# A route's product one step behind its spread, with two tile buffers, and gathers six units ahead

## The chip, the cores and the metric

The kernel runs on one core of a Trainium2 chip. The metric is device time in microseconds of one execution, from the first to the last instruction with what lies around them; smaller is better. Engines are named as in the profile: PE (TensorE, with PEld for its weight loads), DVE (VectorE), ACT (ScalarE), POOL (GpSimd) and SP (SyncE).

## The reference

```python
N, deg, C, L, DE = 10000, 64, 64, 1, 4      # nodes, mean degree, channels
E = N * deg                                 # 640000 edges
M = (L + 1) ** 2                            # 4 components

def reference(x, src, dst, Y, edge_feat, w_rad, cg, w_mix):
    N, C, M = x.shape[0], x.shape[1], x.shape[2]
    R = _silu(edge_feat @ w_rad)                              # (E, C)
    xs = x[src]                                               # (E, C, M)
    tp = jnp.einsum('eci,ef,ifo->eco', xs, Y, cg)             # (E, C, M)
    msg = R[:, :, None] * tp
    agg = _segment_sum(msg.reshape(-1, C * M), dst, N).reshape(N, C, M)
    return jnp.einsum('ncm,cd->ndm', agg, w_mix)
```

`src` and `dst` are random node numbers, `Y` and `edge_feat` have 4 numbers for each edge, and all data is float32.

## The kernel before

The work is to sort the edges by destination, so that the edges of 32 destination nodes (a bucket) lie together, and then to gather the source rows and add the messages up by matmuls. The edges are taken in two parts, 49% and 51%. Each edge is carried as 9 words (a key of source and destination, `Y`, `edge_feat`).

**Two sorting passes.** Pass 1 (`pass1`, key `grp`) puts a part's edges into 18 groups of 576 nodes; pass 2 (`pass2`, key `bkt`) puts a group's edges into its 18 buckets. Both use `route`, which works on chunks of 12 tiles of 128 edges. Its steps for chunk `k`:

- `prepare`, `places`, `placed`, `slots` find each edge's row and slot, for two chunks at a time (DVE one-hots, PE prefix matmuls, ACT and DVE on their result).
- `spread` (L445 to L467) builds the tiles `X` (the edge's words at its slot, DVE, L453) and `oh` (one-hot of its row: seven of twelve by DVE, L460, five by ACT, L465 and L466). They are rotating buffers; `self.xb` says how many.
- `move` (L469) multiplies them on PE into PSUM: 12 float32 matmuls, recorded as 24 (L473).
- `evict` (L476) copies the PSUM tile to `rt` on ACT (L478). There are `rt_bufs` of them: 6 in the main phase.
- `store` (L480) writes the rows out by an indirect DMA that POOL issues (L481).

In step `k` of the loop, `evict(k-3)` and `move(k-2)` come first and `spread(k)` after them. In the main phase `grp` has two buffers of `X` and `oh`, and `bkt` has three. In the sort of the first part, ahead of the main phase, there are three.

Before a route can start, its table has to be there. In pass 1 `front` counts digits: for each block of 24 tiles a DVE one-hot `Da` (L543), a PE count `cnt` (L546) and, a step later, a DVE addition to `cs` (L550). After that `tables` runs as a chain of short DVE, PE and ACT operations, among them `offp` (L313), `ovp` (L363) and `dp` (L380). PE's results of these share one PSUM bank (`misc`) with the last mixing product `po` (L795); `bank()` hands it out. `weave` lays the next front's steps between the steps of the running route.

**Messages** (`messages`, L668). A unit is half of a bucket's edges in a part: 4 tiles in the first part, 5 in the second; each part has 313 buckets, so 626 units. For unit `k` POOL issues one gather for each tile (L709, into `xg`, with `LG + 2` buffers, `LG` units ahead). PE transposes the payload (`turn`, L722) and makes the radial product (`radial`, L732), and ACT applies SiLU (L735). DVE builds the selection `S` (`spots`, L742 and L745) and multiplies the gathered rows in place (`products`, L752). PE adds up (`sums`, L763). Every fourth bucket is mixed by `wf` (L795) and written out. A unit's work is issued in four quarters:

```python
        quarters = (((index, LI), (gather, LG), (turn, 2), (sums, 0), (silu, 1)), ((turned, 2), (spots, 1)),
                    ((products, 1), (evict, 0)), ((radial, 2), (full, -1)))
```

The PSUM tile of `turn(k+2)` is the one that `products(k)` reads last.

**The order.** `run` first sorts part 0 by pass 1. The main phase, `groups` (L830), then goes through all 36 segments (part and group). Between the quarters of the messages it deals out steps of pass 2 for the next segment (`pass2_steps` over the quarters of the present one) and steps of pass 1 of part 1 (`rate` steps for each quarter, up to the last segment of part 0). In the main phase the program order of PE, DVE and ACT is as written; the scheduler orders POOL and SP by its own reckoning. Each engine works its queue off in order. After the main phase two short loops treat edges that had no place (`overflow`).

Of the kernel before, what the change touches and what calls it, by code (L numbers as in the profile page):

```python
# [17 lines left out]
F = mybir.dt.float32  # L18
# [6 lines left out]
P = 128  # L25
# [7 lines left out]
BT = 18  # L33
UT = 5
SPLIT = ((0.49, 2, 4), (0.51, 2, 5))
LG = 4
LI = 8
LS = 8
BIG = 16384.0
# [30 lines left out]
class Kernel:  # L70
# [320 lines left out]
    def route(self, ps, quad, nt, sb, idx):  # L391

        nc, wk, tc, T, Q = self.nc, self.ph, self.tc, ps.T, ps.Q
        assert Q == 2
        N = (nt + T - 1) // T
        QD, PS, PP, MS, XO, PR, RT = {}, {}, {}, {}, {}, {}, {}

        def prepare(q):
            QD[q] = quad(q * Q * T, min(Q * T, nt - q * Q * T))

        def places(q):
            t0 = q * Q * T
            m = min(Q * T, nt - t0)
            pp = self.ps.tile([P, 28, B], F, name="pp", tag="pos", bufs=1)
            Dq = QD[q][0]
            for c in range((m + T - 1) // T):
                a, z = c * T, min((c + 1) * T, m)
                nc.tensor.matmul(pp[:, a:z, :], ps.identr[:N, q * Q + c:q * Q + c + 1].to_broadcast([N, P]),
                                 sb[:N, :].unsqueeze(1).to_broadcast([N, z - a, B]),
                                 start=(c == 0), stop=False)  # L410
            full = m // T
            if full:
                po = pp[:, :full * T, :].rearrange("p (c t) b -> p c t b", t=T)
                pi = Dq[:, :full * T, :].rearrange("p (c t) b -> p c t b", t=T)
                for u in range(T - 1):
                    k = T - 1 - u
                    nc.tensor.matmul(po[:, :, u + 1:, :], self.onesb,  # L417
                                     pi[:, :, u:u + 1, :].to_broadcast([P, full, k, B]), start=False, stop=False)
            for u in range(full * T, m - 1):
                nc.tensor.matmul(pp[:, u + 1:m, :], self.onesb, Dq[:, u:u + 1, :].to_broadcast([P, m - u - 1, B]),  # L420
                                 start=False, stop=False)
            nc.tensor.matmul(pp[:, :m, :].rearrange("p t b -> p (t b)"), self.A,
                             Dq.rearrange("p t b -> p (t b)"), start=False, stop=True)
            PS[q] = pp

        def placed(q):
            m = min(Q * T, nt - q * Q * T)
            pp = PS.pop(q)
            pc = PP[q] = wk.tile([P, Q * T, B], F, name="pc", tag="pc" + ps.key, bufs=1)
            nc.scalar.activation(pc[:, :m, :], pp[:, :m, :], AF.Copy, bias=-BIG)  # L430

        def slots(q):
            pp = PP.pop(q)
            m = min(Q * T, nt - q * Q * T)
            pos = wk.tile([P, 28], F, name="pos", tag="pos" + ps.key)
            nc.vector.tensor_reduce(pos[:, :m], pp[:, :m, :], axis=AX.X, op=OP.max)
            ri = wk.tile([P, 28], I32, name="row", tag="row" + ps.key)
            nc.vector.tensor_scalar(ri[:, :m], pos[:, :m], 1.0 / ps.r, 0.5 / ps.r - 0.5, op0=OP.mult, op1=OP.add)
            row = wk.tile([P, 28], F, name="rowf", tag="rowf" + ps.key)
            nc.vector.tensor_copy(row[:, :m], ri[:, :m])  # L440
            slot = wk.tile([P, 28], F, name="slot", tag="slot" + ps.key)
            nc.vector.scalar_tensor_tensor(slot[:, :m], row[:, :m], -float(ps.r), pos[:, :m], op0=OP.mult, op1=OP.add)
            MS[q] = (row, slot)

        def spread(c):  # L445
            row, slot = MS[c // Q]
            a = (c % Q) * T
            m = min(T, nt - c * T)
            msk = self.vmsk[:, :m * ps.r].rearrange("p (t s) -> p t s", s=ps.r)
            nc.vector.tensor_tensor(msk, self.v128[:, :ps.r].unsqueeze(1).to_broadcast([P, m, ps.r]),  # L450
                                    slot[:, a:a + m].unsqueeze(2).to_broadcast([P, m, ps.r]), op=OP.is_equal)
            X = self.ph.tile([P, T, ps.rw], F, name="X", tag="X" + ps.key, bufs=self.xb[ps.key])
            nc.vector.tensor_tensor(  # L453
                X[:, :m, :].rearrange("p t (s w) -> p t s w", w=W),
                msk.unsqueeze(3).to_broadcast([P, m, ps.r, W]),
                QD[c // Q][1][:, a:a + m, :].unsqueeze(2).to_broadcast([P, m, ps.r, W]), op=OP.mult)
            oh = self.ph.tile([P, T, P], F, name="oh", tag="oh" + ps.key, bufs=self.xb[ps.key])
            v = max(m - ps.act, 0)
            if v:
                nc.vector.tensor_tensor(oh[:, :v, :], self.v128.unsqueeze(1).to_broadcast([P, v, P]),  # L460
                                        row[:, a:a + v].unsqueeze(2).to_broadcast([P, v, P]), op=OP.is_equal)
            if m - v:
                sq = self.ph.tile([P, 5, P], F, name="sq")
                for u in range(v, m):
                    nc.scalar.activation(sq[:, u - v, :], self.i128, AF.Square, bias=row[:, a + u:a + u + 1], scale=-1.0)  # L465
                nc.scalar.activation(oh[:, v:m, :], sq[:, :m - v, :], AF.Relu, bias=self.ones[:, 0:1], scale=-2.0)  # L466
            XO[c] = (X, oh, m)  # L467

        def move(c):  # L469
            X, oh, m = XO.pop(c)  # L470
            pr = self.ps.tile([P, 512], F, name="pr", tag="route", bufs=2)
            for u in range(m):
                nc.tensor.matmul(pr[:, :ps.rw], oh[:, u, :], X[:, u, :], start=(u == 0), stop=(u == m - 1))  # L473
            PR[c] = pr

        def evict(c):  # L476
            rt = RT[c] = self.ph.tile([P, ps.rw], F, name="rt", tag="rt" + ps.key, bufs=self.rt_bufs)
            nc.scalar.activation(rt, PR.pop(c)[:, :ps.rw], AF.Copy)  # L478

        def store(c):  # L480
            st = nc.gpsimd.indirect_dma_start(  # L481
                out=ps.dst, out_offset=bass.IndirectOffsetOnAxis(ap=idx[:, c:c + 1], axis=0),
                in_=RT.pop(c), in_offset=None, bounds_check=ps.rows - 1, oob_is_err=False)
            if self.in_group[ps.key]:
                tc.declare_no_dep(st.ins, group=ps.key, reason="the rows of a pass are apart")
            tc.add_to_no_dep_group(ps.key, st.ins)
            self.in_group[ps.key] += 1


        for k in range(-2 * Q, N + LS):  # L490
            if 0 <= k - 3 < N:
                evict(k - 3)
            if 0 <= k - 2 < N:
                move(k - 2)
            if k % 2 and 0 <= k + 3 < N:

                while self.pos:
                    yield "held"
                self.pos = True
                places((k + 3) // 2)  # L500
            if k % 2 == 0 and 0 <= k + 2 < N:
                placed((k + 2) // 2)
                self.pos = False
            if k % 2 == 0 and 0 <= k + 4 < N:
                prepare((k + 4) // 2)
            if 0 <= k < N:
                spread(k)
            if (k + 1) % 2 == 0 and 0 <= k + 1 < N:
                slots((k + 1) // 2)
            if 0 <= k - LS < N:  # L510
                store(k - LS)
            yield

    def pass1(self, part, first, size):
# [16 lines left out]
        def front(o, m):  # L531
# [8 lines left out]
            for a in range(0, m, QT):  # L540
                z = min(a + QT, m)
                D = ph.tile([P, QT, B], BF, name="Da", bufs=2)
                self.onehot(D[:, :z - a], da[:, a:z], z - a)  # L543
                yield from self.bank()
                cnt = self.ps.tile([P, 512], F, name="cnt", tag="misc", bufs=1)
                self.count(cnt, ps, D, a // T, z - a, N, True, True)  # L546
# [283 lines left out]
    def groups(self):  # L830
# [11 lines left out]

        total = max(ends[self.NG - 2] - 8, 1) if self.NG > 1 else 1
        nch = (self.part[1][1] - self.part[1][0] + self.p1.T - 1) // self.p1.T
        rate = (nch + 6 * (LS + 4) + 60) / total
        acc = acc1 = 0.0
        i = start = 0
        for v in range(4 * u):
# [106 lines left out]
    def run(self):  # L955
# [2 lines left out]
        self.segs = [(k, g) for k in range(2) for g in order]  # L958
        with tile_pool(name="p1", bufs=2) as self.ph:
            self.rt_bufs = 38  # L960
            self.xb = {"grp": 3}
            self.z = self.ph.tile([P, 2048], F, name="z", bufs=1)
            nc.gpsimd.memset(self.z, 0.0)
            self.consts()
# [9 lines left out]
                run(weave(first, later, 0.25))  # L974
        with tile_pool(name="p2", bufs=2) as self.ph:
            self.rt_bufs = LS - 2
            self.xb = {"grp": 2, "bkt": 3}
            with self.tc.manual_schedule(engines={mybir.EngineType.PE, mybir.EngineType.DVE,
                                                  mybir.EngineType.Activation}):
                self.groups()  # L980
# [32 lines left out]
```

## Time and profile before

| | |
|---|---|
| median of 3 runs | 10404.88 us (10403.27 to 10411.17) |
| profiled execution | 10414.15 us, its span 10412.3 us |
| mean granted TensorE clock | 0.883 |
| pass 1 of part 0, table and sort of the first segment | 0 to about 1130 us |
| main phase with pass 1 of part 1 in it | 1130 to about 5550 us |
| main phase with pass 2 alone beside the messages, last units of part 0 | 5550 to about 6010 us |
| the same, units of part 1 | 6010 to 10256 us |
| end of the last units, overflow loops | 10256 to 10412 us |

A row of the waits names the engine and line that waited, what it waited for, the total in microseconds, how often, and the longest. A row of the groups gives busy time and mean nanoseconds of one, then the idle time before and what ended it. A row of the timeline gives start, duration, engine, line, operation, tiles and shapes, a count where neighbours are merged, and idle time before it in brackets.

### The profile page before, as it was taken

The numbers are of one execution on the slowest core, as the hardware profiler recorded it, in microseconds if no ns is written. First come the engines' busy times: TensorE is split into PE (matmuls) and PEld (weight loads), VectorE is DVE, ScalarE is ACT, GpSimd is POOL, SyncE is SP. The second block draws the span as 40 slices with busy tenths as digits, with TensorE's granted clock in tenths as the row PEclk, the third lists the DMA queues.
The fourth block names the chain that finished last, engine by engine and source line by source line (L and its number), as shares of the span: only waits on it lengthen the run. The fifth ranks groups of instructions, "written<-read, shape, count | busy, mean of one in ns | idle before, by whom it ended". The sixth has DMA issues, their size and how long they took to land. (4 is left out here: it accounts for less than half of the span.)

```text
span 10412.3 us, 159949 instructions
## 1 busy us (share of the span) xinstructions
PE 8505.1 (82%) x58324; PEld 7273.0 (70%) x58324; DVE 7312.6 (70%) x12462; ACT 3587.7 (34%) x11277; POOL 6285.0 (60%) x6576
## 2 busy tenths in 40 slices
PE   6897878778888778878889888888888888888874
PEld 5786767667667667667767677777767777777663
DVE  8998877677677677677767676666666666666643
ACT  3675433233334233334433232222222232332210
POOL 1222655546456446456557777777777777777773
PEclk9998989889889789889889898888899898888986
DMA  3331322223223223223223333333333333333331
GB/s 95 85 91 51 93 74 82 78 64 92 68 71 96 70 65 97 64 70 93 78 76 104 109 109 113 111 112 111 112 112 112 112 111 112 111 111 111 109 112 52
DMA packets 531585, 963.05 MB, mean 92 GB/s; under 512 B 229053, under 2 KB 329720, under 8 KB 530800
## 3 DMA queue, kind: packets, MB, share of 16 engines
q0 software_dynamic: 300464, 790.37, 26.0%
q1 hardware_dynamic: 227744, 149.89, 5.4%
q10 hardware_dynamic: 2592, 12.60, 0.3%
q8 instruction: 459, 7.52, 0.3%
q14 instruction: 326, 2.67, 0.1%
HBM read 830.53 MB, written 131.52 MB: 92 GB/s over the span
## 5 line engine op out<-in xcount | busy, mean ns | idle before, releaser
L709 POOL DMA_INDIRECT xg<-in_x_dram,sidx x5634 | 5359.0, 951 | 2576.7 <-issue 1494.7
L763 PE MATMUL G<-S,xg 128*128 128x128 f32 x22536 | 3329.7, 313 | 5.8 <-DVE dv L742 2.7
L763 PEld LDWEIGHTS G<-S,xg 128*128 128x128 f32 x22536 | 3218.0, 228 | 24.1 <-issue 4.2
L473 PE MATMUL pr<-X,oh 128*128 128x126 f32 x21180 | 2644.8, 282 | 148.1 <-DVE oh L460 85.9
L473 PEld LDWEIGHTS pr<-X,oh 128*128 128x128 f32 x21180 | 2525.4, 197 | 278.6 <-DVE oh L460 97.5
L752 DVE TENSOR_TENSOR xg<-xg,pre 128x1024 f32<-128x1024 f32 (+1 forms) x1252 | 1689.0, 1349 | 1403.3 <-DMA xg<-in_x_dram,sidx 1130.9
L453 DVE TENSOR_TENSOR X<-dv,Wt 128x1512 f32<-128x1512 f32 (+2 forms) x905 | 1531.4, 1692 | 892.0 <-PE pr L473 846.1
L465 ACT ACTIVATE sq<-i,rowf 128x128 f32<-128x128 f32 x4457 | 1397.6, 393 | 60.0 <-DVE rowf L440 49.4
L722 PE MATMUL pre<-ident,pay 128*36 128x128 f32 (+1 forms) x1252 | 402.3, 321 | 1034.8 <-DVE xg L752 1013.2
L735 ACT ACTIVATE pre<-pre 128x256 f32<-128x256 f32 (+1 forms) x1252 | 494.0, 395 | 2000.7 <-PE pre L732 1944.9
L722 PEld LDWEIGHTS pre<-ident,pay 128*36 128x36 f32 (+1 forms) x1252 | 141.0, 113 | 1473.3 <-DVE xg L752 1299.2
L745 DVE TENSOR_TENSOR S<-dv,pay 128x512 f32<-128x512 f32 (+1 forms) x1252 | 949.3, 758 | 223.2 <-PE G L763 133.0
L732 PE MATMUL pre<-wr,sT 36*128 36x256 f32 (+1 forms) x2504 | 1024.4, 492 | 13.6 <-ACT sT L727 13.6
L481 POOL DMA_INDIRECT grp<-rt,idx x417 | 412.5, 989 | 959.2 <-ACT rt L478 563.3
L466 ACT ACTIVATE oh<-sq,ones 128x640 f32<-128x640 f32 (+1 forms) x905 | 740.0, 818 | 620.8 <-PE pr L473 602.1
L460 DVE TENSOR_TENSOR oh<-dv,rowf 128x896 f32<-128x896 f32 x887 | 948.1, 1069 | 0.0
L727 ACT ACTIVATE sT<-pre 36x128 f32<-36x128 f32 (+1 forms) x1252 | 332.4, 265 | 1570.1 <-PE pre L722 1568.3
L481 POOL DMA_INDIRECT bkt<-rt,idx x488 | 487.1, 998 | 458.6 <-ACT rt L478 280.3
L795 PE MATMUL po<-wf,Gs 128*128 128x256 f32 (+2 forms) x2784 | 681.0, 400 | 65.9 <-DVE cs L550 63.5
L795 PEld LDWEIGHTS po<-wf,Gs 128*128 128x128 f32 (+2 forms) x2784 | 509.2, 188 | 227.9 <-DVE cs L550 68.9
L780 ACT ACTIVATE Gs<-G 128x128 f32<-128x128 f32 x1252 | 276.0, 272 | 1068.8 <-PE G L763 1068.7
L417 PE MATMUL pp<-D,onesb 128*128 128x396 bf16 (+14 forms) x4983 | 540.7, 257 | 12.6 <-DVE D L284 12.6
(176 smaller groups left out, 5041.4 us busy)
## 6 DMA issues: line engine op xcount, KB each, us to landing
xg<-in_x_dram,sidx POOLq DMA_INDIRECT x5634
bkt<-z SPq DMA_DIRECT2D x26, 972.0 KB
out_dram<-ot SPq DMA_DIRECT2D x138, 128.0 KB
pay<-bkt SPq DMA_DIRECT2D x17, 810.0 KB
grp<-z SPq DMA_DIRECT2D x17, 738.0 KB
Wt<-grp SPq DMA_DIRECT2D x17, 738.0 KB
grp<-z ACTq DMA_DIRECT2D x17, 706.5 KB
Wt<-grp SPq DMA_DIRECT2D x17, 706.5 KB
```

What stands on the lines that cost most here:

```text
L453: nc.vector.tensor_tensor(X[:, :m, :].rearrange("p t (s w) -> p t s w", w=W), msk.unsqueeze(3).to_broadcast([P, m, ps.r, W]), QD[c // Q][1 ...
L460: nc.vector.tensor_tensor(oh[:, :v, :], self.v128.unsqueeze(1).to_broadcast([P, v, P]), row[:, a:a + v].unsqueeze(2).to_broadcast([P, v, P ...
L465: nc.scalar.activation(sq[:, u - v, :], self.i128, AF.Square, bias=row[:, a + u:a + u + 1], scale=-1.0)
L466: nc.scalar.activation(oh[:, v:m, :], sq[:, :m - v, :], AF.Relu, bias=self.ones[:, 0:1], scale=-2.0)
L473: nc.tensor.matmul(pr[:, :ps.rw], oh[:, u, :], X[:, u, :], start=(u == 0), stop=(u == m - 1))
L481: st = nc.gpsimd.indirect_dma_start(out=ps.dst, out_offset=bass.IndirectOffsetOnAxis(ap=idx[:, c:c + 1], axis=0), in_=RT.pop(c), in_offset ...
L709: nc.gpsimd.indirect_dma_start(out=xg[:, t, :], out_offset=None, in_=self.x, in_offset=bass.IndirectOffsetOnAxis(ap=si[:, u:u + 1], axis=0))
L732: nc.tensor.matmul(R, ST_.pop(k)[:ut * W], self.wr[:ut * W, :ut * 64], start=True, stop=True)
L745: nc.vector.tensor_tensor(S[:, :ut], self.eq[:, :ut].unsqueeze(3).to_broadcast([P, ut, NB, 4]), pb[:, :, 1:5].unsqueeze(2).to_broadcast([P ...
L752: nc.vector.tensor_tensor(V, V, R.unsqueeze(3).to_broadcast([P, ut, 64, 4]), op=OP.mult)
L763: nc.tensor.matmul(G[:, h].rearrange("p n f -> p (n f)"), V[:, t, 32 * h:32 * h + 32, :].rearrange("p c i -> p (c i)"), S[:, t].rearrange( ...
L795: nc.tensor.matmul(po[:nn, :256], Gs[:, h, f].rearrange("p b n -> p (b n)")[:, :nn], self.wf[:, h, f, :], start=(h + f == 0), stop=(h + f ...
```

## The change

- `self.xb` becomes one number for both passes: 3 in the first sort, 2 in the main phase. The distance from spread to product is `lag = xb - 1`: two steps in the first sort, as it was, and one step in the main phase. The eviction stays one step behind the product.
- In `front` a `yield` stands between the block's one-hot and its count, so that the two are a step apart. The rate at which pass 1 of part 1 is dealt out counts 80 further steps instead of 60.
- `LG` is 6 instead of 4: gathers are issued 6 units ahead, into 8 buffers instead of 6.

```diff
-LG = 4
+LG = 6
...
-            X = self.ph.tile([P, T, ps.rw], F, name="X", tag="X" + ps.key, bufs=self.xb[ps.key])
+            X = self.ph.tile([P, T, ps.rw], F, name="X", tag="X" + ps.key, bufs=self.xb)
...
-            oh = self.ph.tile([P, T, P], F, name="oh", tag="oh" + ps.key, bufs=self.xb[ps.key])
+            oh = self.ph.tile([P, T, P], F, name="oh", tag="oh" + ps.key, bufs=self.xb)
...
+        lag = self.xb - 1
         for k in range(-2 * Q, N + LS):
-            if 0 <= k - 3 < N:
-                evict(k - 3)
-            if 0 <= k - 2 < N:
-                move(k - 2)
+            if 0 <= k - lag - 1 < N:
+                evict(k - lag - 1)
+            if 0 <= k - lag < N:
+                move(k - lag)
...
                 self.onehot(D[:, :z - a], da[:, a:z], z - a)
+                yield
                 yield from self.bank()
                 cnt = self.ps.tile([P, 512], F, name="cnt", tag="misc", bufs=1)
...
-        rate = (nch + 6 * (LS + 4) + 60) / total
+        rate = (nch + 6 * (LS + 4) + 80) / total
...
-            self.xb = {"grp": 3}
+            self.xb = 3
...
-            self.xb = {"grp": 2, "bkt": 3}
+            self.xb = 2
```

## The prediction

> **What bounds the kernel now.** I read the page first, then the busy times by stretch, then the waits of each engine inside the stretch that the change touches, then the timeline.
>
> ```profile
> span 10412.3 us, 159949 instructions
> PE 8505.1 (82%) x58324; PEld 7273.0 (70%) x58324; DVE 7312.6 (70%) x12462; ACT 3587.7 (34%) x11277; POOL 6285.0 (60%) x6576
> ...
> 700.00:800.00 100.00, 94.47 (x821) 86.38 (x820) 98.59 (x186) 76.58 (x229) 25.16 (x26) 1.00 0.26 86
> ...
> 1130.00:5550.00 4420.00, 3633.66 (x24723) 3107.61 (x24721) 3150.63 (x5478) 1594.13 (x5115) 2441.89 (x2545) 0.87 0.27 79
> 5550.00:6010.00 460.00, 388.42 (x2677) 330.06 (x2678) 326.39 (x556) 153.41 (x498) 342.00 (x359) 0.91 0.37 106
> 6010.00:10256.00 4246.00, 3535.05 (x23384) 3002.43 (x23384) 2752.70 (x4069) 1177.02 (x3695) 3214.92 (x3370) 0.89 0.38 112
> ```
>
> The rows by stretch give length, then busy time (count) of PE, PEld, DVE, ACT, POOL, then PE's clock. No engine is full on average, but the stretches differ. The sort of the first half (the row at 700) is DVE's: 98.59 of 100. From 1130 to 5550 three things are woven: messages of the first half, pass 2, and pass 1 of the second half. I call it stretch 1; nobody is full there: PE is idle for 4420 − 3634 = 786 us, DVE for 1269. From 5550 on pass 1 is over, and from 6010 (stretch 3) the second half's messages run.
>
> ```profile
> POOL xg L709 <- PE G L763: 773.5, 237, 12.7
> POOL xg L709 <- issue: 531.1, 1727, 3.4
> ...
> L481 POOL DMA_INDIRECT grp<-rt,idx x213 | 214.0, 1005 | 201.0 <-ACT rt L478 88.0 <-issue 44.8 <-DVE S L745 16.0
> L481 POOL DMA_INDIRECT bkt<-rt,idx x210 | 208.7, 994 | 292.5 <-ACT rt L478 230.7 <-issue 22.6 <-DVE S L745 8.2
> ...
> DVE xg L752 <- DMA xg<-in_x_dram,sidx: 1005.3, 304, 6.7
> ```
>
> The first four rows are waits and groups of stretch 1, the last is a wait of stretch 3. Between two gathers lie 531.1 / 1727 = 0.31 us of issue, so one indirect DMA takes 342.00/359 + 0.31 = 1.26 us of POOL. 3370 of them make 4246 us: exactly stretch 3. There POOL is full, its end is POOL's, and DVE's 1005 us of waiting for gathers only show it. In the 460 us before, 359 × 1.26 = 452: full too. So time can be won in stretch 1 alone, and there 773.5 us of POOL's slack (waiting for a gather buffer, that is, for the sums) are the most that can go before POOL is full as well: 4420 − 773 = 3647.
>
> Why PE idles in stretch 1, and what DVE and ACT wait for there:
>
> ```profile
> PE pre L722 <- DVE xg L752: 322.2, 121, 10.1
> PE cnt L291 <- DVE Da L284: 195.2, 61, 11.2
> PE po L795 <- DVE cs L550: 63.5, 23, 3.1
> PE ovp L363 <- DVE rk L360: 53.2, 10, 11.7
> PE pr L473 <- ACT rt L478: 47.2, 64, 3.6
> PE offp L313 <- DVE R L310: 35.9, 9, 8.0
> PE dp L380 <- DVE val L377: 32.0, 8, 6.4
> ...
> PE pr L473 <- DVE oh L460: 0.4, 1, 0.4
> ...
> DVE X L453 <- PE pr L473: 832.4, 204, 10.6
> ...
> DVE xg L752 <- DMA xg<-in_x_dram,sidx: 38.3, 21, 2.9
> ...
> ACT oh L466 <- PE pr L473: 602.1, 185, 15.3
> ```
>
> The seven long rows of PE come to 749 of its 786 us, and six of them wait for DVE. DVE, which is busy only 71% of the stretch, comes late because it stood 832 us at X, 204 times, about once for each of the 213 pass 1 chunks: with two buffers, the spread of chunk k overwrites what the product of k−2 reads, and that product is queued in the very same step. ACT stands there too (602), and the SiLU and the evictions queue behind it.
>
> **The change, part by part.**
>
> *Product one step behind, two buffers.* For pass 1 the product of k−2 now stands one step before spread k. The code deals pass 1 out at (213 + 72 + 60)/2308 = 0.149 steps a quarter unit, one in 6.7 quarters; 530 units in 4420 us are 8.34 us a unit, 2.08 a quarter, so the step is 14 us ahead, more than the longest wait of 10.6. Most of the 832 and 602 go. For pass 2 (three buffers, two steps, to two buffers, one step) the overwrite distance stays one step. What is late next is PE itself: DVE's idle time is worth only what PE waits for DVE. Of the 322.2 at the transpose (it stands before the sums, and both need the product of DVE) I let 60% go, −190 (bounds 0 and −322): of DVE's 1269 idle us 832, 66%, lie at X, and part of its lateness is its own bursts of work. Of the chain waits (63.5 + 53.2 + 35.9 + 32.0 = 184.6), where PE waits for short DVE operations behind a backlog, half, −90 (bounds 0 and −185). The 47.2 for the PSUM buffer stays, since the eviction moves up with the product; a chunk's output tile is still reused six chunks later, and its store keeps its place.
>
> *What it can cost: the product waiting for its own spread.* At lag one the product takes the place that the product of the chunk before has now. Three pass 2 chunks of the timeline:
>
> ```profile
> 3045.66 1.73 DVE L453 TENSOR_TENSOR X<-dv,Wt 128x1512 f32<-128x1512 f32 x1
> 3047.31 1.08 DVE L460 TENSOR_TENSOR oh<-dv,rowf 128x896 f32<-128x896 f32 x1
> 3048.82 0.69 DVE L745 TENSOR_TENSOR S<-dv,pay 128x512 f32<-128x512 f32 x1
> 3049.43 1.21 DVE L752 TENSOR_TENSOR xg<-xg,pre 128x1024 f32<-128x1024 f32 x1
> 3050.56 0.33 DVE L450 TENSOR_TENSOR dv<-dv,slot 128x168 f32<-128x168 f32 x1
> 3052.18 2.84 PE L473 MATMUL pr<-X,oh 128*128 128x126 f32 x24
> 3052.65 1.08 DVE L460 TENSOR_TENSOR oh<-dv,rowf 128x896 f32<-128x896 f32 x1
> 3058.19 1.08 DVE L460 TENSOR_TENSOR oh<-dv,rowf 128x896 f32<-128x896 f32 x1
> 3059.09 2.84 PE L473 MATMUL pr<-X,oh 128*128 128x126 f32 x24
> 3064.10 2.94 PE L473 MATMUL pr<-X,oh 128*128 128x126 f32 x24
> ...
> PE pr L473 <- DVE oh L460: 83.8, 104, 9.1
> ```
>
> The spreads end at 3048.39, 3053.73 and 3059.27; the products one place ahead start at 3052.18, 3059.09 and 3064.10: 3.8, 5.4 and 4.8 us later. So the spread would be in time. Bounds: 0.4 us in all (stretch 1 at lag two, row above) and the last row, the first sort, where DVE is full: 83.8 us for 204 chunks, 0.41 each, for 423 chunks 174. I take +30, near the lower end.
>
> *The yield between the count's one-hot and its matmul.* The count now stands a step (14 us) behind DVE's one-hot instead of right at it: of 195.2 us (61 waits, 3.2 each) 20 stay, −175 (bounds 0 and −195). The longer front takes 10 to 20 more steps a piece; the pace goes from 345 to 365 per 2308 quarters, so pass 1 ends where it did.
>
> *PE's clock.* A wait is paid twice:
>
> ```profile
> 3012.76 1.95 PE L763 MATMUL G<-S,xg 128*128 128x128 f32 x16
> ...
> 3017.47 0.29 PE L722 MATMUL pre<-ident,pay 128*36 128x128 f32 x1 [2.14 <-DVE xg L752]
> 3017.60 2.92 PE L763 MATMUL G<-S,xg 128*128 128x128 f32 x16
> ...
> L763 PE MATMUL G<-S,xg 128*128 128x128 f32 x8480 | 1291.8, 318 | 1.0 <-ACT Gs L780 1.0
> L473 PE MATMUL pr<-X,oh 128*128 128x126 f32 x9814 | 1246.5, 286 | 48.0 <-ACT rt L478 47.2 <-DVE oh L460 0.4
> ```
>
> The same sums took 1.95 us, and 2.92 after a wait of 2.14. The granted clock was 0.87 in stretch 1 with PE idle 18%, and 1.00 at 700 to 800 with PE idle 6%. At full clock 530 units of sums would be 530 × 1.95 = 1034 instead of 1291.8, and 9814/24 = 409 products of 2.84 us 1161 instead of 1246.5: 343 us slow time beside 786 idle, 0.44 for each. The net of the parts so far, −190 − 90 + 30 − 175 = −425, brings −185 more (bounds 0 and −343). The Trainium skill (TensorE: Matmul & The Clock Gate, Part 1: The HAM clock gate) lets the clock fall only after an idle window of about 3.4 us; the mean wait, 322.2/121 = 2.7, is shorter, and by that the −185 would be nothing. The row with 2.14 us speaks against it here.
>
> *POOL fills up.* 4420 − 610 = 3810 against POOL's 3647: 96% full. DVE's wait for gathers is 38.3 us now, at 83%, and 1005.3 where POOL is full. I take +120 (bounds 0 and 1005 × 3810/4246 = 902), near the lower end, since two more units lie ready.
>
> *Gathers 6 ahead, 8 buffers.* The SBUF of one X and one-hot set becomes two gather buffers. In stretch 1 it adds nothing beyond that; at its end POOL is 2 units, 8 gathers × 1.26 = 10 us, further on, and since POOL alone counts from there, −10 at the end. A store that POOL's queue holds behind two more units of gathers lands 2 × 4246/626 = 13.6 us later in stretch 3, and ACT's evictions, with the SiLU queued behind them, may then wait for an output tile. The 4246 − 3535 = 711 us that PE is idle there cover that; without this cover, 13.6 us in each of 17 groups would be 231.
>
> *First sort.* It keeps three buffers and lag two. Its third front is now longer than the route it is woven into (some 107 steps, of which the weave deals out 0.72 × 106 = 76), so part of it and the table chain may lie open:
>
> ```profile
> 1022.35 0.50 DVE L306 TENSOR_REDUCE n<-cs 14x18 f32<-14x216 f32 x1 [1.00 <-ACT cs L653]
> 1040.02 0.18 DVE L387 TENSOR_SCALAR idx<-dest 128x14 int32<-128x14 f32 x1 [0.65 <-ACT dest L384]
> ```
>
> An open table chain took 18 us. I take +15 (0 to 26).
>
> **Sum.** Stretch 1: −425 − 185 + 120 = −490. With −10 and +15: −485. The profiled execution took 10414.15 us (span 10412.3 and 1.9 around it): 9929. The median of the runs, 10404.88, lies 9 below it: **9920 us**.
>
> **Rivals.** (1) *DVE's wait only moves*: freed at X, DVE waits elsewhere for PE, and PE's transposes wait as before; only the counts gain, −175 × 1.44 = −252: 10150. For it: DVE was never full. Against: the late DVE rows. (2) *POOL becomes the bound in stretch 1*: all of its 773 go: 10405 − 773 − 10 + 15 = 9637. It needs nearly all PE idle time to vanish. (3) *Slower: products wait for their spreads.* A group's sort is paced to 52 steps (6 + 14 + 8 + 24) in the 144 quarters of 36 units, so a pass 2 step is 2.77 × 2.08 = 5.8 us. If DVE has spots, product and a pass 1 spread (0.69 + 1.21 + 3.14, the last being 0.33 + 1.73 + 1.08) in front of its own 3.14, it takes 8.2: 2.4 us of waiting for each of 210 chunks, 504, with the clock's 1.44 726: 10405 − 485 + 726 = 10646. It ends slower than before when the mean wait exceeds 485/(210 × 1.44) = 1.6 us. Against: the 3.8 to 5.4 us above. (4) *No difference*: gains and costs cancel, or stretch 1 is paced by something these views do not show: 10405.
>
> **Numbers.** Forecast 0.60, rival 1 0.18, rival 2 0.08, rival 3 0.10, rival 4 0.04. A measurement of this kernel tells about 0.2% (21 us) from no change. Faster: 0.60 + 0.18 + 0.08 = 0.86; same 0.04; slower 0.10. The range leaves out rivals 3 and 4 and the extreme of 2: 9660 (near POOL's bound) to 10290 (rival 1 with half of its gain).
>
> **What would show it.** Right: DVE at X waiting for PE falls from 832 to under 200 and ACT's 602 likewise; the count's 195 under 40; PE's clock in stretch 1 above 0.87; that stretch near 3930 us; POOL's wait for the sums under 350; stretch 3 still 4246 within 1%. Wrong: PE's product waiting for one-hots by over 300 us; the transposes still at 300; or stretch 3 longer, POOL idle in it behind a store.

## The result, and the profile after

The changed kernel takes 9529.29 us (median of 4 runs, 9524.70 to 9534.47) against 10408.02 (4 runs of the kernel before): ratio 0.9156, 95% interval 0.914 to 0.9172. The gain is 879 us where 485 were forecast, and the time lies below the range's lower end of 9660. The forecast had the side and the place right. It missed the size, and one of its steps, POOL filling up, did not happen.

The page after: span and busy time, then PE's granted clock in 40 slices, and two groups.

```profile
span 9532.7 us, 160093 instructions
PE 8150.8 (86%) x58324; PEld 6981.4 (73%) x58324; DVE 7320.2 (77%) x12462; ACT 3565.7 (37%) x11277; POOL 6272.6 (66%) x6576
...
PEclk9999799999999999999998898898889888888986
...
L453 DVE TENSOR_TENSOR X<-dv,Wt 128x1512 f32<-128x1512 f32 (+2 forms) x905 | 1531.6, 1692 | 156.1 <-PE pr L473 100.8
...
L466 ACT ACTIVATE oh<-sq,ones 128x640 f32<-128x640 f32 (+1 forms) x905 | 740.2, 818 | 22.8
```

The work is the same (the counts on every engine are those of before), yet PE is busy 354 us less (8505.1 before): it does the same matmuls at a higher clock. ACT's wait for PE at `oh`, 602 us in stretch 1 before, is gone altogether.

To compare the same units I divided both executions by them: stretch 1 is now from the end of DVE's product of unit 10 to that of unit 540, which the timeline puts at 1134.6 and 5553.6 us before and at 1153.0 and 4676.0 after. So 4419 us became 3523. Busy time by stretch (length, then PE, PEld, DVE, ACT and POOL, PE's clock, DMA share and GB/s), before:

```profile
1134.60:5553.60 4419.00, 3633.39 (x24721) 3107.61 (x24721) 3151.64 (x5480) 1594.10 (x5114) 2441.20 (x2544) 0.87 0.27 79
5553.60:6276.00 722.40, 614.99 (x4251) 523.23 (x4251) 510.48 (x834) 233.76 (x753) 538.08 (x564) 0.92 0.38 109
6276.00:10261.00 3985.00, 3308.62 (x21803) 2809.72 (x21804) 2567.26 (x3788) 1095.34 (x3435) 3017.11 (x3163) 0.89 0.38 111
```

and after:

```profile
1153.00:4676.00 3523.00, 3242.11 (x24405) 2789.66 (x24403) 3107.40 (x5382) 1557.12 (x5030) 2427.32 (x2533) 0.96 0.35 99
4676.00:5350.00 674.00, 605.77 (x4334) 517.31 (x4335) 522.29 (x862) 249.05 (x806) 489.26 (x514) 0.93 0.37 105
5350.00:9379.00 4029.00, 3347.09 (x22027) 2834.05 (x22027) 2592.53 (x3821) 1093.32 (x3464) 3049.65 (x3205) 0.89 0.39 112
```

All of the gain is in the first row. PE's idle time there fell from 786 to 281 us, its busy time from 3633 to 3242, and the clock rose from 0.87 to 0.96. Behind it hardly anything changed: from unit 626 to the last, 4213.8 us before and 4195.1 after.

The units are the same in both first rows, the work of pass 1 is not quite. Before, the row held the stores of all 213 chunks of pass 1 that fall into the main phase; after, it holds 201:

```profile
L481 POOL DMA_INDIRECT grp<-rt,idx x201 | 201.8, 1004 | 101.6 <-issue 41.5 <-ACT rt L478 31.0 <-DVE val L356 6.1
```

The other 12 now run behind unit 540, the last of them in unit 559 instead of 532. The prediction's remark that pass 1 ends where it did was wrong.

PE's waits in stretch 1 after:

```profile
PE pre L724 <- DVE xg L754: 187.6, 90, 11.6
PE ovp L363 <- DVE rk L360: 40.7, 11, 9.1
PE pr L473 <- DVE oh L460: 15.8, 13, 2.8
PE offp L313 <- DVE R L310: 10.2, 7, 3.1
PE dp L380 <- DVE val L377: 7.5, 5, 3.2
PE pr L473 <- ACT rt L478: 5.2, 7, 1.2
...
PE cnt L291 <- DVE Da L284: 1.6, 1, 1.6
```

and those of DVE and POOL there:

```profile
DVE xg L754 <- ACT pre L737: 93.1, 77, 4.3
DVE S L747 <- PE G L765: 74.3, 47, 5.5
DVE X L453 <- PE pr L473: 53.0, 29, 4.2
...
DVE xg L754 <- DMA xg<-in_x_dram,sidx: 21.1, 11, 5.2
...
POOL xg L711 <- issue: 541.3, 1759, 2.9
POOL xg L711 <- PE G L765: 168.9, 134, 6.5
POOL bkt L481 <- ACT rt L478: 87.1, 45, 8.7
...
POOL grp L481 <- ACT rt L478: 31.0, 16, 7.5
```

DVE stands 53 us at X where it stood 832, the counts no longer wait (195.2 to 1.6), and the product waits 15.8 us for its own one-hots. The stores' wait for ACT's evictions, which holds up the gathers behind them in POOL's queue, fell from 319 to 118.

### The profile page after: what moved, and what is told of

Read it like the earlier page. It is cut to its first block, busy times and chain, and to the rows that moved or that the text cites. A ratio compares the mean times of both kernels' runs of the same rounds, so it can differ in the third digit from the quotient of the medians.

```text
span 9532.7 us, 160093 instructions
## 1 busy us (share of the span) xinstructions
PE 8150.8 (86%) x58324; PEld 6981.4 (73%) x58324; DVE 7320.2 (77%) x12462; ACT 3565.7 (37%) x11277; POOL 6272.6 (66%) x6576
## 5 line engine op out<-in xcount | busy, mean ns | idle before, releaser
L765 PE MATMUL G<-S,xg 128*128 128x128 f32 x22536 | 3109.3, 300 | 4.4 <-DVE dv L744 2.5
L765 PEld LDWEIGHTS G<-S,xg 128*128 128x128 f32 x22536 | 3000.7, 216 | 24.7 <-issue 3.2
L473 PE MATMUL pr<-X,oh 128*128 128x126 f32 x21180 | 2602.5, 280 | 150.9 <-DVE oh L460 113.7
L473 PEld LDWEIGHTS pr<-X,oh 128*128 128x128 f32 x21180 | 2478.1, 195 | 285.8 <-DVE oh L460 112.2
L734 PE MATMUL pre<-wr,sT 36*128 36x256 f32 (+1 forms) x2504 | 979.1, 472 | 34.1 <-ACT sT L729 34.0
```

The lines of the kernel that those rows point to most:

```text
L734: nc.tensor.matmul(R, ST_.pop(k)[:ut * W], self.wr[:ut * W, :ut * 64], start=True, stop=True)
L765: nc.tensor.matmul(G[:, h].rearrange("p n f -> p (n f)"), V[:, t, 32 * h:32 * h + 32, :].rearrange("p c i -> p (c i)"), S[:, t].rearrange( ...
```

## The experiments

The series fell on chips of two kinds. On chips of the first kind the kernel before takes 10404 to 10408 us, as in the profile above (A below, more than one chip); on two others it takes 12078 and 11903 (B and C). A ratio is always to the kernel before of the same series.

**Which part carries the gain.** The first series, on B, split the change.

`lag_only` keeps the distance and the buffers and undoes the rest of the changed kernel:

```diff
-LG = 6
+LG = 4
...
-                yield
...
-        rate = (nch + 6 * (LS + 4) + 80) / total
+        rate = (nch + 6 * (LS + 4) + 60) / total
```

> Product one step behind and two buffers for both passes; no yield in the fronts, 4 gathers ahead. Theory A (a wait of PE removed is worth itself and 0.77 of itself in clock): of the 505 us of PE idle that went from stretch 1, the 194 of the counts stay, 311 go, times 1.77 is 550: about 9860 us, counts still waiting 150 to 200 us. Rival B (the six units of gathers made the difference): gain under 200 us, above 10200. Rival C (the parts need each other, since DVE's backlog at the counts is the backlog at X): the counts' wait falls here without the yield, below 100 us, and the time comes to 9700 or less.

`yield_only` is the kernel before with the yield and the 80:

> Kernel before with only the yield in the fronts and the rate of 80. Theory A: the counts' 195 us of PE idle fall below 30 us; times 1.77 that is 310 at most, and as DVE still stands at X 832 us part of it turns up at the transposes: 10080 to 10250, 10130 as one number. Rival C: PE waits for DVE elsewhere instead, gain below 60 us.

`lg4` is the changed kernel with `LG = 4`:

> The changed kernel with 4 units of gathers ahead instead of 6. Theory A: 10 us later at the end of stretch 1 and little else: 9530 to 9560. Rival B: POOL runs short in stretch 1 with the shorter lead, DVE's wait for gathers there rises from 21 us to over 150, and the time is above 9650.

`p1_lag1` gives each pass its own distance in the kernel before:

```diff
+        lag = self.lag[ps.key]
-            if 0 <= k - 3 < N:
-                evict(k - 3)
-            if 0 <= k - 2 < N:
-                move(k - 2)
+            if 0 <= k - lag - 1 < N:
+                evict(k - lag - 1)
+            if 0 <= k - lag < N:
+                move(k - lag)
...
+            self.lag = {"grp": 1, "bkt": 2}
```

> Kernel before with only pass 1's product one step behind (two buffers); pass 2 keeps three buffers and two steps, 4 gathers ahead, no yield. Theory A: the overwrite wait of pass 1 is the whole of the 832 us at X, so this equals the run with both passes at one step within 40 us: about 9860. Rival D (pass 2's shorter distance costs, by products that wait for their one-hots): this one is faster than that by over 40 us. Rival E (ACT and DVE waited in pass 2 too): slower by over 40 us.

Measured, before 12077.89: `lag_only` 11393.73 (0.9439, 0.9423 to 0.9454), `yield_only` 11770.73 (0.9749, 0.9733 to 0.9766), `lg4` 11289.41 (0.9347, 0.933 to 0.9363), `p1_lag1` 11384.02 (0.9434, 0.9415 to 0.9453). Pass 1's distance alone gives what both give, so it is pass 1's overwrite that cost. The yield (with the 80) alone saves 307 us, but on top of the distance only 104 (11394 to 11289): the parts are not additive. `after_b`, the changed kernel itself, and `lg4_b` ran together on B later:

> The changed kernel itself, as the measure for the others of this series: ratio to before 0.914 to 0.917 where the kernel before takes 10400 us.

> The changed kernel with 4 units of gathers ahead. Theory A: 10 us at the end of stretch 1 and little else: 10 to 40 us above the changed kernel. Rival B (POOL runs short with the shorter lead): DVE's wait for gathers in stretch 1 rises from 21 us to over 100 and the time by over 100.

11288.96 and 11281.95, ratios 0.9348 (0.9332 to 0.9364) and 0.9341 (0.9324 to 0.9357): on B six units ahead instead of four are worth nothing. `lag_only_b`, of the same series, came to 11408.91 (0.9448).

> Product one step behind and two buffers alone (no yield, 4 ahead). The run without the yield but with 6 ahead took 9583. Theory A: this is 10 to 40 us above it, 9595 to 9625, ratio 0.922 to 0.925, so that the distance carries over nine tenths of the whole gain. Rival B: above 9700.

`no_yield` ran on A; it is the changed kernel without the yield and with 60:

> The changed kernel without the yield in the fronts and with the rate of 60; 6 gathers ahead and one step of distance stay. Theory A (waits add up, each worth itself and its share of clock): the counts' 195 us of PE idle come back, ratio to before 0.945 to 0.95. Theory C (the backlog at X was also the backlog at the counts): with X free, DVE is early at the counts too, they wait under 120 us, ratio 0.925 to 0.94.

9583.01 against 10407.30: 0.921 (0.9194 to 0.9225). That is theory C's side, a little beyond its range. PE's waits in its stretch 1 (the units 10 to 540 end at 1137.4 and 4761.6):

```profile
PE pre L723 <- DVE xg L753: 119.5, 68, 7.4
PE cnt L291 <- DVE Da L284: 69.5, 44, 11.7
```

Without any yield the counts' wait fell from 195.2 to 69.5: they had waited mostly because DVE stood at X with the count's one-hot queued behind. The yield and the 80 together are worth 54 us (9583.01 to 9529.29, two series). What the yield takes from the counts, 68 us, comes back at the transposes, where PE waits 119.5 us without it and 187.6 with it. The two runs also differ in the work: here all 213 chunks of pass 1 lie in stretch 1, in the changed kernel 201. No run has the yield without that shift.

`lag_only_c` (on C) and `lag_only_d` (on A) repeat the distance alone:

> One step of distance and two buffers alone (no yield, 4 ahead). Without the yield but with 6 ahead it was 9583 where before took 10407. Theory A: 10 to 40 us above that, 9595 to 9625, ratio 0.922 to 0.925: the distance carries nine tenths of the gain. Rival B (the lead of the gathers carries much of it): above 9700.

> One step of distance and two buffers alone (no yield, 4 ahead). Where the kernel before takes 10400 us: theory A 9595 to 9625, rival B (the gathers' lead carries much) above 9700. On a chip where it takes 11900 or more: ratio 0.944 to 0.947, as before.

On C 11261.15 (0.9465, 0.9449 to 0.9481). On A 9644.98 against 10404.34: 0.9269 (0.9254 to 0.9285), between the two theories there, and where `lag_only` had put its rival C (9700 or less, the counts' wait below 100 us). The row of its stretch 1, and rows of its PE and POOL there:

```profile
1136.00:4789.60 3653.60, 3309.30 (x24721) 2845.71 (x24721) 3156.85 (x5481) 1590.75 (x5114) 2435.88 (x2544) 0.95 0.34 95
...
PE pre L723 <- DVE xg L753: 130.4, 73, 7.6
PE cnt L291 <- DVE Da L284: 69.9, 42, 11.7
...
POOL bkt L481 <- ACT rt L478: 201.5, 81, 6.9
...
POOL grp L481 <- ACT rt L478: 12.3, 7, 3.2
```

With exactly the records of before (24721) PE is idle 344 us instead of 786 and busy 324 us less. So on A the distance alone gives 759 us; six ahead 62 more (9644.98 to 9583.01, two series whose kernels before differ by 3), not 10 to 40; the yield with its 80 gives 54 more. Of the 62, 32 fall in units 100 to 540 (3036.8 to 3004.5 us), where DVE's wait for gathers went from 30 to 10.

`p2_lag1` is the counterpart: only pass 2 at one step, with two buffers.

```diff
+            self.lag = {"grp": 2, "bkt": 1}
-            self.xb = {"grp": 2, "bkt": 3}
+            self.xb = {"grp": 2, "bkt": 2}
```

> Kernel before with only pass 2's product one step behind and with two buffers; pass 1 keeps two steps and two buffers, with its overwrite wait. The prediction's slower rival alone: 0.1 to 0.2 us for each of 457 chunks by the slack seen in the profile before, 0 to 50 us slower than before (ratio 1.000 to 1.005); by the rival's price 504 to 726 us slower. Pass 2's two-step distance with three buffers was worth nothing if it is within 20 us.

On C 11917.04 against 11903.16: 1.0003 (0.9991 to 1.0015). With the distances set as in `p1_lag1`, this takes pass 2 alone: its second step of distance, and the third buffer that it needed, were worth nothing there.

**Does POOL's filling up cost anything?** `pool_load` gave POOL a memset ahead of each unit's gathers:

```diff
+            if g[0] == 0:
+                idle = ph.tile([P, 256], F, name="idle", bufs=1)
+                nc.gpsimd.memset(idle, 0.0)
```

> The changed kernel with one extra POOL memset of 256 floats a partition ahead of each unit's gathers in the first part (626 of them, d us each; it serves nothing). Prediction's theory (POOL is nearly full in stretch 1): the time rises by at least 0.8 x 626 x d. Theory A (POOL's slack in stretch 1 is real, its waits for the sums and for output tiles shrink by what it is given): the rise is below 0.4 x 626 x d, mostly from the last 86 units of the first part, where POOL is full.

9678.85 against 10407.30 (0.9302, 0.9287 to 0.9318), 150 us more than the changed kernel. But this run doesn't tell the theories apart: nothing tied the memsets to their units, and the timeline has all 626 of them between 965 and 1448 us. Units 0 to 100 and what precedes them took 147 us longer, and units 100 to 540 took 2939 us against 2935. `pool_load2` writes the same amount into the unit's own gather buffer, in the slot that four-tile units leave free:

```diff
+            if g[0] == 0:
+                nc.gpsimd.memset(xg[:, ut, :], 0.0)
```

> The changed kernel with a POOL memset of 256 floats a partition in each unit of the first part, into the fifth slot of the unit's own gather buffer, which that part does not use; so it can't run ahead of the buffer (626 of about 0.34 us with the step to the next, 213 in all, 180 of it in units 20 to 540). Prediction's theory (POOL nearly full in stretch 1): units 20 to 540 take 144 us or more longer than in the changed kernel. Theory A (POOL's waits there are slack that shrinks): below 70 us longer there; the 86 units after it take 30 longer in both.

> The changed kernel with a POOL memset of 256 floats a partition in each unit of the first part, in the fifth slot of the unit's own gather buffer (0.34 us each with the step to the next; 440 of them, 150 us, in units 100 to 540). Prediction's theory (POOL nearly full in stretch 1, so what it is given goes into the time): units 100 to 540 take 120 us or more above the 2935 of the changed kernel. Theory A (POOL's waits there are slack): 60 us or less above it. On the other chip it was 47 of 150.

> The changed kernel with a POOL memset of 256 floats a partition in each unit of the first part, in the fifth slot of the unit's own gather buffer (0.34 us each with the step to the next; 150 us of it in units 100 to 540). Where the kernel before takes 10400 us: by the prediction's theory units 100 to 540 take 3055 us or more (2935 in the changed kernel), by theory A 2995 or less. On a chip where it takes 11900 or more, the 47 of 150 seen before.

On B 11348.63 (0.9395, 0.9379 to 0.9411), 60 above `after_b`, with 47 of it in units 100 to 540; on C 11218.85 (0.9429), without the changed kernel beside it. On A 9547.43 (0.9179, 0.9164 to 0.9194), and there it settles the point. The memset's row, then POOL's waits, of stretch 1 of `pool_load2_d`:

```profile
L710 POOL MEMSET xg<- x626: 306/332/433, 963.0 to 5168.6; 128x256 f32 x157
...
POOL bkt L481 <- ACT rt L478: 60.1, 32, 6.6
...
POOL xg L710 <- PE G L767: 23.9, 6, 6.4
...
1153.00:4676.00 3523.00, 3235.42 (x24339) 2782.68 (x24338) 3107.46 (x5364) 1551.67 (x5014) 2596.61 (x3051) 0.96 0.35 98
```

440 units with 0.34 us more of POOL each, 150 us, took 2946.3 us instead of 2935.1. POOL's waits for the sums (168.9 to 29) and for ACT's evictions (118 to 81) took up the rest. On A POOL is not a bound of stretch 1, not even when it has 150 us more to do.

**Is a gap of PE paid twice?** `pe_fill` puts useless matmuls behind the radial product of each unit of the first part, in the kernel before:

```diff
+            if units[k][0][0] == 0:
+                for _ in range(6):
+                    nc.tensor.matmul(pre[:, 256:384], self.onesb, self.onesb, start=True, stop=True)
```

> Kernel before with six bf16 matmuls of 128 columns behind each radial product of the first part (into 128 unused columns of its PSUM tile): 626 x about 0.5 us of PE work that serves nothing and shortens PE's gaps. Theory A (a gap lowers PE's clock for what follows): the sums of stretch 1, 318 ns a pass in the kernel before, fall below 305 ns, the granted clock rises above 0.89, and the time grows by less than 150 us of the 310 of added work. Rival F (the clock does not depend on gaps of this size): sums stay at 315 to 320 and the time grows by 200 us or more.

10439.33 against 10407.30: 1.0035 (1.002 to 1.0049). Two groups of its stretch 1 (1134.6 to 5587), then that stretch:

```profile
L767 PE MATMUL G<-S,xg 128*128 128x128 f32 x8492 | 1236.1, 308 | 0.6 <-ACT Gs L784 0.6
...
L736 PE MATMUL pre<-onesb 128*128 128x128 bf16 x3182 | 291.3, 232 | 0.0
...
1134.60:5587.00 4452.40, 3737.71 (x27916) 3212.02 (x27914) 3152.64 (x5480) 1592.13 (x5116) 2436.80 (x2546) 0.89 0.27 78
```

In the stretch 291 us of added matmuls raised PE's busy time by 104 and the length by 33. The sums went from 318 to 308 ns (below 305 was expected) and the clock from 0.87 to 0.89. This supports theory A: work put into the gaps made the other matmuls faster. PE's idle time fell by 71 us, and the time that the trace has at half clock fell from 1137 to 942 us. PE's wait at the transposes fell from 322 to 243.

**What is late next.** DVE is busy 3107 of 3523 us after the change, ACT 1557. `act6` moves one more of twelve one-hots from DVE to ACT:

```diff
-        self.p1 = Pass(T, r, 1 << (cap + P - 1).bit_length(), cap, 5)
+        self.p1 = Pass(T, r, 1 << (cap + P - 1).bit_length(), cap, 6)
...
-        self.p2 = Pass(T, r, 1 << (cap + P - 1).bit_length(), cap, 5)
+        self.p2 = Pass(T, r, 1 << (cap + P - 1).bit_length(), cap, 6)
...
-                sq = self.ph.tile([P, 5, P], F, name="sq")
+                sq = self.ph.tile([P, 6, P], F, name="sq")
```

> The changed kernel with six of a chunk's twelve one-hots on ACT instead of five (both passes). DVE was 88% busy in stretch 1 after the change, ACT 44%. Theory A (DVE is now what PE waits for): one-hots on DVE 1.08 to 0.93 us, in the first sort 204 x 0.15 = 31 us, in stretch 1 PE's 188 us at the transposes fall by 30 to 60: 0.5 to 1.1% below the changed kernel. Rival (ACT becomes late with its SiLU, 0.4 us more for each chunk): DVE waits for ACT at the products above 150 us in stretch 1 and the time is not below that of the changed kernel.

9472.47 against 10407.30: 0.9106 (0.9091 to 0.9121), 57 us below the changed kernel (two series) and the fastest on A. 29 us come from the first sort (the first product ends at 1075.5 instead of 1104.6) and 26 from units 100 to 540; PE's wait at the transposes went from 188 to 174, less than the 30 to 60 us expected, and DVE's for ACT at the products from 93 to 106. `act7` moves two:

> The changed kernel with seven of twelve one-hots on ACT (both passes). Six took 9472 against 9529: 29 us in the first sort, 26 in units 100 to 540. Theory A (DVE still carries both): another 25 to 50 us, 9420 to 9450. Rival (ACT, 77 us more busy in the first sort than with six, becomes late): 9465 or more, with DVE waiting for ACT at the products above 130 us in stretch 1.

It ran on C: 11129.27, 0.9355 (0.934 to 0.9371). Neither the changed kernel nor `act6` ran there, so whether seven beat six stays open. DVE's wait for ACT at the products, expected above 130 if ACT became late, was 526 from unit 10 to 540; but on C that wait is long with five one-hots on ACT as well (374 in `pool_load2_c`, 576 in `lag_only_c`), so it does not tell.

## Why the prediction was right and wrong

*What bounds the kernel.* Right. The time came out of stretch 1 alone, and stretch 3 kept POOL's pace: 3205 indirect DMAs in 4029 us, 1.26 us each.

*Product one step behind.* Right in mechanism. DVE at X fell to 53 us (under 200 was named), ACT's 602 to nothing. `lag_only_d` shows the part by itself: the transposes gave 192 us (190 forecast), the chain waits 108 of 184.6 (90 forecast), and the product waited 27.3 us for its own spread (30 forecast). What the forecast left out were the counts, which gave 125, and the wait for the PSUM buffer, which I let stay and which fell from 47.2 to 17.8. So this part took 441 us of PE's idle time where −250 stood. Rival 3 was not there, and `p2_lag1` on C measured pass 2's side of it by itself at no difference.

*The yield.* This term failed. The counts' row went to 1.6 us, but `no_yield` shows that freeing X took 126 of the 195 already, and that the transposes wait 68 us longer with the yield. Beyond the two other parts, the yield took 53 us of PE's idle time (333 to 281) where −175 stood. Most of it was one lateness of DVE that showed in both rows. Nor did pass 1 end where it did: its last store moved from unit 532 to unit 559.

In all PE's idle time fell by 505 us where −425 was the net: 80 of the miss. That these are so close is partly luck, since the first part was put 191 us too small and the yield 122 too large.

*PE's clock.* The mechanism holds, the term was too small: −185 forecast, while PE's busy time fell by 354 over the whole kernel with the same instructions. In stretch 1 it fell by 343 in `no_yield`, whose records there are those of before (24727 against 24721), and by 391 in the changed kernel, which has 316 fewer records there. I priced slow time in two groups only, the sums and the products, 343 us, and scaled it by idle time. The sums alone gave back 189 of their 258:

```profile
L765 PE MATMUL G<-S,xg 128*128 128x128 f32 x8484 | 1103.1, 287 | 0.0
L473 PE MATMUL pr<-X,oh 128*128 128x126 f32 x9558 | 1166.4, 280 | 26.0 <-DVE oh L460 15.8 <-ACT rt L478 5.2 <-ACT sq L465 4.0
...
L734 PE MATMUL pre<-wr,sT 36*128 36x256 f32 x1062 | 377.2, 436 | 3.3 <-ACT sT L729 3.3
```

The radial products, 419.9 before and 377.2 now, and the mixing products, 308.6 and 276.9, were slow too. With the distance alone a microsecond of idle time removed brought 324/441 = 0.73 of clock, not 0.44.

That is no fixed price. The trace has the granted clock at full or at half, in pieces of whole multiples of 3.41 us. In stretch 1 it was at half 172 times before, 1137 us together; 57 times and 345 us in `lag_only_d`; 44 times in `no_yield` (294 us) and in the changed kernel (300 us). So the 53 us of idle time that went with the yield brought no clock. Taken by periods of 3.41 us at full clock, before: all 135 in which PE was idle 60% or more were followed by half clock, 37 of the 62 between 40 and 60%, and none of the 763 below 40%. What counted was how much of such a period was idle.

The Trainium skill lets the clock fall after an idle window of about 3.4 us (TensorE: Matmul & The Clock Gate, Part 1: The HAM clock gate). The trace agrees on the length but not that the whole of it must be idle: 91 of the 172 periods before a drop touch no gap of PE as long as that. The prediction set that window beside the mean wait of 2.7 us, which decides little either way, since its rows hold waits of up to 11.7 us.

*POOL fills up.* This step failed. I took POOL's time without its waits for the sums, 3647 us, as its need, and added 120 for gathers that come late when it is 96% full. The 3647 held 319 us in which POOL's stores waited for ACT's evictions, which are not need: 214 were left in `lag_only_d`, where ACT no longer stands at `oh`, and 118 with all parts. Stretch 1 came to 3523, below that bound, and DVE's wait for gathers fell to 21. `pool_load2_d` shows directly that 150 us more of POOL cost 11 there. So rival 2 was priced by a wrong bound: its 9637 was no floor, and neither was the range's 9660, which rested on it. (At the range's other end, half of rival 1's gain of 252 gives 10279 and not 10290.)

*Six ahead.* −10 was forecast from POOL's lead at the end of stretch 1; `lag_only_d` against `no_yield` gives 62 without the yield on A (two series on different chips), half of it inside units 100 to 540, and `lg4_b` against `after_b` nothing on B. With the yield, on A, it was not run alone. The new wait for output tiles in stretch 3 came as described, and PE's idle time covered it. The row is ACT's, from 4840 to 9379:

```profile
ACT rt L478 <- DMA bkt<-rt,idx: 341.1, 81, 8.9
```

*First sort.* Forecast +15; the first product of the messages ends at 1104.6 instead of 1102.5. What was lost came behind it: units 0 to 20 took 113 us instead of 84, and 75 without the yield.

In sum: stretch 1 fell by 406 us more than forecast (896 gone, 490 forecast). POOL's term is 120 of it, the idle time 80, and PE's busy time 206. Of these 206, 158 are the clock by `no_yield` (343 against 185). The other 49 came with the yield and the 80, at the same time at half clock and with 12 chunks of pass 1 fewer in the stretch; that these chunks are all of it is not shown.

## What to carry to other kernels

When an engine stands at an overwrite, look for what else is queued behind it: here one wait of DVE and ACT was also most of the counts' wait (125 of 195 us) and part of the wait for the PSUM eviction (29 of 47) and of POOL's stores (105 of 319). It was no part of DVE's wait for the SiLU, 158 us before and 168 with the distance alone. Price such parts together, because a wait that two edits both address goes only once. In an engine's time, count only its work as need; its waits move with the wait that is removed, so a bound that holds them is none. Price PE's gaps with all of its matmuls, not only with the largest groups, and look at whether they gather within a few microseconds.

## What the runs showed of the hardware

On A, the clock of PE in the kernel before fell to half behind every period of 3.41 us in which PE was idle 60% or more, and behind none in which it was idle less than 40% (135 of 135 and 0 of 763 such periods in stretch 1), whether or not a single gap filled the period. After the change it was 29 of 29 and 1 of 891.

On B and C the kernel before takes 14 to 16% longer than on A, and the profile shows a difference that has no cause in it. PE pauses between matmuls of one accumulation where it waits for nothing, and others see its results late. PE and then ACT in `after_b`, on B:

```profile
8012.96 0.27 PE L724 MATMUL pre<-ident,pay 128*45 128x128 f32 x1
8013.07 0.72 PE L765 MATMUL G<-S,xg 128*128 128x128 f32 x5
8013.97 0.27 PE L765 MATMUL G<-S,xg 128*128 128x128 f32 x1 [0.18 <-issue]
8014.68 1.82 PE L765 MATMUL G<-S,xg 128*128 128x128 f32 x14 [0.44 <-issue]
...
8014.95 0.27 ACT L729 ACTIVATE sT<-pre 45x128 f32<-45x128 f32 x1 [4.09 <-remote]
```

The transpose is done at 8013.23, and ACT, idle for 4.09 us, starts on it at 8014.95. Waits put down to nothing that the profile shows come to 675 us on PE in that run and to 7 in the changed kernel's run on A. POOL is not full there in stretch 3 (1330 indirect DMAs from 7000 to 9000 us against 1592). The change gives 6.5% on B and 8.4% on A. Why these chips do this, and whether that is why the gain is smaller there, the runs don't show.
